# Weaving the P V of an older tile into the scores of a newer one, piece by piece, in a decode attention kernel

## The chip, the cores and the metric

The kernel runs on one core of a Trainium2 chip. The metric is the device time of one execution in microseconds (us), as the median of several executions. Engines carry the names of the profile: PE is TensorE (matmuls), PEld its weight loads, DVE VectorE, ACT ScalarE, SP SyncE, which here only issues transfers (DMAs).

## The reference, cut to what matters

One decode step: four sequences, 32 heads, 8192 cached keys and values of 128 numbers for each, in bf16. K and V together are 537 MB, and every byte is read once.

```python
B, Sq, D = 4, 1, 512
H, Sk, Dh = 32, 8192, 128
...
q = (x @ wq).reshape(B, Sq, H, Dh).transpose(0, 2, 1, 3)
scores = einsum("bhqd,bhkd->bhqk", q, k_cache) * (Dh ** -0.5)
p = softmax(scores)
o = einsum("bhqk,bhkd->bhqd", p, v_cache)
return x + o.transpose(0, 2, 1, 3).reshape(B, Sq, H * Dh) @ wo + FFN(layernorm(x))
```

## The kernel before

K and V come in 32 tiles each of 8.39 MB (four heads of one sequence). A tile fills one of three large slots. VectorE transposes a K tile in 32 pieces, TensorE multiplies each piece twice (64 matmuls of 512 columns a tile: the scores), and later multiplies P by V in 64 chunks of 512 columns (P V). The weights of a score matmul are 128 rows by 128 columns, those of a P V matmul 128 rows by 16 columns; every matmul loads its own.

```python
NSLOT = 3
slots   = ctx.enter_context(tc.tile_pool(name="slots", bufs=NSLOT))
kt_pool = ctx.enter_context(tc.tile_pool(name="ktp", bufs=3))
# ... (cut)
def t_piece(n, g, jb):                      # VectorE: one piece of K turned
    kt = kt_pool.tile([P, w // 2], dt.bfloat16, name="kt")
    nc.vector.transpose(out=kt[:]..., in_=src[:, :, jb, :])

def s_piece(n, g, jb):                      # TensorE: its scores, two matmuls
    for r in range(2):
        mm(s_ps[n][:], zq[:, 2 * jb + r, off:off + P], kt[:, :, r], ...)

def pv_chunk(n, k):                         # TensorE: one chunk of P V
    w = HT * NV                             # 16 columns of weights
    mm(o_acc[j % 2][b * QB:b * QB + w, :], pt[n][:, off:off + (w - 1) * QB + 1:QB],
       v_tiles[n][:, k * 512:(k + 1) * 512], start=(k == 0))
# ... (cut)
for i in range(NT):
    for g in range(NTG):
        for jb in range(2):
            t_piece(i, g, jb); s_piece(i, g, jb)      # all scores of tile i
        if g == 1 and i > 0:
            pt_turn(i - 1)                            # P of the tile before, transposed
    # ...
    load_v(i)                # into the slot that K(i) leaves
    max_1(i); build_q(i + 1)
    for k in range(NK):
        pv_chunk(i - 1, k)   # then all of P V of tile i - 1
        if k == 8:
            max_2(i)         # maximum, exp
    row_sums(i)
    load_k(i + 2)            # into the slot that V(i - 1) leaves
    if bv == B - 1:
        fin_1(jv); fin_q(jv) # every fourth tile: division by the row sums
```

## Time and profile before

| | before |
|---|---|
| median of the timed runs | 1304.13 us (1302.58 to 1304.63) |
| span in the profile | 1305.5 us |
| DMA share and rate, 2 to 1189 us | 1.00, 431 GB/s |
| PE busy | 87% of the span |
| mean spacing of K loads, tiles 4 to 31 | 39.3 us |
| two transfers of 8.39 MB at 431 GB/s | 38.9 us |

The two last rows are nearly equal: a stage (one tile's scores and one tile's P V) takes as long as its bytes. The prediction below shows the lines for that. One place in the same trace, which it does not show, became important afterwards. It is the change from scores to P V in the timeline of the kernel before (columns: start, duration, engine, line, operation, output and input, count, and in brackets the idle time before it and what ended it):

```profile
720.12 1.20 PE L75 MATMUL sps<-kt,zq 128*128 128x512 bf16 x4
...
720.71 0.10 PEld L75 LDWEIGHTS <-zq 128*128 128x128 bf16 x1 [0.27 <-issue]
721.25 1.64 PEld L75 LDWEIGHTS <-ptz 128*16 128x16 bf16 x9 [0.44 <-issue]
721.25 2.13 PE L75 MATMUL oacc<-slot,ptz 128*16 128x512 bf16 x9
```

Inside a run of one kind the matmuls start 0.216 us apart, and the next weights are loaded while a matmul runs. At the change the first weight load of P V starts at 721.25, together with its own matmul, 0.44 us after the load before it had ended. The records under these lines give starts of 720.934 for the last score matmul, 721.249 for the first P V matmul and 721.489 for the second: 0.315 and 0.240 us. So the change costs 0.315 + 0.240 - 2 x 0.216 = 0.12 us.

### The profile page before, as it was taken

The numbers are of one execution on the slowest core, as the hardware profiler recorded it, in microseconds if no ns is written. First come the engines' busy times: TensorE is split into PE (matmuls) and PEld (weight loads), VectorE is DVE, ScalarE is ACT, GpSimd is POOL, SyncE is SP. The second block draws the span as 40 slices with busy tenths as digits, with TensorE's granted clock in tenths as the row PEclk, the third lists the DMA queues.
The fourth block names the chain that finished last, engine by engine and source line by source line (L and its number), as shares of the span: only waits on it lengthen the run. The fifth ranks groups of instructions, "written<-read, shape, count | busy, mean of one in ns | idle before, by whom it ended". The sixth has DMA issues, their size and how long they took to land.

```text
span 1305.5 us, 12271 instructions
## 1 busy us (share of the span) xinstructions
PE 1136.1 (87%) x4725; PEld 463.8 (36%) x4788; DVE 807.9 (62%) x1509; ACT 35.0 (3%) x79; POOL 3.6 (0%) x11
## 2 busy tenths in 40 slices
PE   1898888988889988889988889988889988889889
PEld 0244333333333333333333333333333333333335
DVE  3956555676555676555676555686555776555771
ACT  1000000000000000000000000000000000000000
POOL 1000000000000000000000000000000000000000
PEclk9897999889989899899998899988999889989899
DMA  9999999999999999999999999999999999999985
GB/s 418 418 432 438 432 432 436 428 442 420 446 422 442 428 436 430 436 430 434 432 436 427 428 424 438 424 432 432 414 436 432 430 428 424 436 436 406 409 339 227
DMA packets 12466, 551.56 MB, mean 422 GB/s; under 512 B 1260, under 2 KB 1784, under 8 KB 3064
## 3 DMA queue, kind: packets, MB, share of 16 engines
q1 hardware_dynamic: 12392, 550.77, 98.1%
q8 instruction: 37, 0.61, 0.2%
q14 instruction: 21, 0.17, 0.0%
q10 hardware_dynamic: 16, 0.01, 0.0%
HBM read 550.77 MB, written 0.00 MB: 422 GB/s over the span
## 4 chain that ended last, share of the span: by engine, by line
PE 58%; DVE 20%; issue 18%; DMA 2%; ACT 0%; DVEq 0%; SPq 0%
PE oacc L75 34%; PE sps L75 21%; DVE kt L272 14%; DVE ptz L309 5%; DMA slot<-in_A_k_cache_dram 2%; PE mps L75 1%; PE yo_ps L75 1%; PE xps L75 1%; DVE o L346 1%; PE mps L291 1%; DVE kt L344 0%; ACT kt L343 0%; DVE rcp L319 0%; DVE otn L366 0%; ACT p__385 L300 0%
## 5 line engine op out<-in xcount | busy, mean ns | idle before, releaser
L75 PE MATMUL sps<-kt,zq 128*128 128x512 bf16 x1985 | 635.4, 430 | 133.3 <-DVE kt L272 133.0
L272 DVE STREAM_TRANSPOSE kt<-slot 128x512 uint32<-128x512 uint32 x1024 | 629.5, 678 | 32.8 <-DMA slot<-in_A_k_cache_dram 12.5
L75 PE MATMUL oacc<-slot,ptz 128*16 128x512 bf16 x2016 | 446.9, 380 | 0.0
L75 PEld LDWEIGHTS <-zq 128*128 128x128 bf16 x2048 | 215.7, 105 | 543.4 <-issue 419.6
L75 PEld LDWEIGHTS <-ptz 128*16 128x16 bf16 x2016 | 206.6, 105 | 226.9 <-issue 13.7
L319 DVE RECIPROCAL rcp<-mps 128x4 f32<-128x4 f32 x32 | 5.9, 185 | 363.9 <-PE mps L75 363.9
L285 DVE TENSOR_REDUCE mx<-sps 128x1 f32<-128x512 f32 x32 | 22.1, 692 | 22.4 <-PE sps L75 22.4
L294 DVE TENSOR_REDUCE nm<-mps 128x4 f32<-128x64 f32 x32 | 7.2, 225 | 31.8 <-PE mps L291 31.8
L75 PE MATMUL xps<-rowy,o 128*32 128x4 f32 (+1 forms) x226 | 10.5, 204 | 15.3 <-DVE o L346 15.3
L263 DVE COPY zq<-qt 32x4 bf16<-32x4 bf16 x128 | 21.1, 165 | 1.3
L75 PEld LDWEIGHTS xps<-rowy,o 128*32 128x32 f32 (+1 forms) x226 | 9.8, 154 | 16.0 <-DVE o L346 16.0
L75 PEld LDWEIGHTS mps<-rowb,rs 128*128 128x128 f32 x64 | 9.7, 190 | 14.9 <-issue 12.9
L75 PE MATMUL mps<-rowb,rs 128*128 128x4 f32 x64 | 12.5, 266 | 1.7 <-ACT p__385 L300 1.7
L75 PEld LDWEIGHTS <-slot 128*128 128x128 bf16 (+1 forms) x274 | 11.7, 123 | 6.3 <-DVE slot L191 2.6
L344 DVE TENSOR_TENSOR kt<-kt,rowu 128x512 f32<-128x512 f32 x8 | 5.5, 693 | 11.2 <-ACT kt L343 10.4
L291 PE MATMUL mps<-ident_f,mx 128*128 128x128 f32 x32 | 10.3, 323 | 0.8 <-DVE mx L285 0.8
L291 PEld LDWEIGHTS mps<-ident_f,mx 128*128 128x128 f32 x32 | 4.3, 133 | 14.2 <-issue 12.9
L366 DVE TENSOR_TENSOR otn<-xps,rcp 32x16 bf16<-32x16 f32 x28 | 4.8, 170 | 7.2 <-PE xps L75 5.1
L75 PE MATMUL yo_ps<-slot,otn 128*4 128x256 bf16 x64 | 8.1, 290 | 0.3 <-DVE otn L356 0.3
L346 DVE TENSOR_REDUCE o<-kt 128x128 f32<-128x512 f32 x8 | 8.2, 1022 | 0.3
L343 ACT COPY kt<-oacc 128x512 f32<-128x512 f32 x8 | 4.7, 586 | 96.8 <-PE oacc L75 96.8
L75 PE MATMUL yo_ps<-slot,kt 128*4 128x256 bf16 x28 | 5.8, 402 | 1.6 <-DVE kt L235 1.6
(148 smaller groups left out, 180.0 us busy)
## 6 DMA issues: line engine op xcount, KB each, us to landing
slot<-in_A_v_cache_dram SPq DMA_DIRECT2D x5, 2048.0 KB, 16.4
slot<-in_A_wq_dram SPq DMA_DIRECT2D x1, 4096.0 KB, 12.2
slot<-in_A_v_cache_dram SPq DMA_DIRECT2D x1, 4096.0 KB, 15.8
slot<-in_A_wo_dram SPq DMA_DIRECT2D x1, 3584.0 KB, 19.7
slot<-in_B_w_gate_dram SPq DMA_DIRECT2D x1, 1792.0 KB, 23.7
slot<-in_B_w_up_dram SPq DMA_DIRECT2D x1, 1792.0 KB, 27.5
slot<-in_B_w_down_dram SPq DMA_DIRECT2D x1, 1792.0 KB
slot<-in_A_v_cache_dram SPq DMA_DIRECT2D x1, 1024.0 KB, 19.7
```

The source lines that it names most:

```text
L75: nc.tensor.matmul(out_ap, lhsT=lhsT, rhs=rhs, start=start, stop=True, skip_group_check=True, **kw)
L263: nc.vector.tensor_copy(out=zq[a * QB:(a + 1) * QB, :, XO + a * QB].rearrange("p (j r) -> p r j", r=2), in_=qt[a * QB:(a + 1) * QB, half, ...
L272: nc.vector.transpose(out=kt[:].bitcast(dt.uint32).rearrange("p (t r) -> p t r", r=QB), in_=src[:, :, jb, :])
L285: nc.vector.reduce_max(out=mx[:], in_=s_ps[n][:], axis=AX.X)
L291: nc.tensor.matmul(mps[:, 0:P], lhsT=nmx.pop(n)[:, 0:1].to_broadcast([P, P]), rhs=ident_f[:, :], is_transpose=True, start=True, stop=True, ...
L294: nc.vector.tensor_reduce(out=nm[:], in_=by_row(mps[:, 0:P]), axis=AX.X, op=ALU.max, negate=True)
L309: nc.vector.transpose(out=t_[y * QB:(y + 1) * QB, :, y, :, :].rearrange("p s u x -> p s (u x)"), in_=p_[y * QB:(y + 1) * QB, :].rearrange( ...
L319: nc.vector.reciprocal(out=rcp[j][:, :, b], in_=mps[:, P:P + HT])
L343: nc.scalar.copy(out=o_sb[:].rearrange("p u d -> p (u d)"), in_=o_acc[j % 2][:])
L344: nc.vector.tensor_tensor(out=o_sb[:], in0=o_sb[:], in1=rowu[:].unsqueeze(2).to_broadcast([P, NV, Dh]), op=ALU.mult)
L346: nc.vector.reduce_sum(out=o1[:], in_=o_sb[:].rearrange("p u d -> p d u"), axis=AX.X)
L366: nc.vector.tensor_tensor(out=otn[q0:q1, j * 4:j * 4 + 4, :], in0=xps[q0:q1], in1=r_[q0:q1, y, :].unsqueeze(1).to_broadcast([QB, 4, B]), o ...
```

## The change

The intent: TensorE and VectorE should both work all the time, and less work should stand behind the last byte. Each half of a tile's scores now runs beside half of the P V of an older tile. The first half of K(i) runs beside the rest of V(i-2), the second beside the first part of V(i-1). K(i+1) is issued in the middle of stage i, when V(i-2) has been read. The last V tile lies in halves in two slots, the first one behind wo.

```diff
-    for i in range(NT):
-        for g in range(NTG):
-            for jb in range(2):
-                t_piece(i, g, jb)
-                s_piece(i, g, jb)
-            if g == 1 and i > 0:
+    for i in range(NT - 1):
+        for p in pieces(i, 0, HP):
+            if i >= 3:
+                pv_to(i - 2, NK // 2 + 2 * p)
+            if i != 2 and i > 0:
+                if p == 4:
+                    max_2(i - 1)
+                if p == HP - 2:
+                    row_sums(i - 1)
+        if i >= 3:
+            load_k(i + 1)
+        for p in pieces(i, HP, NP):
+            if p == 2 and i > 0:
                 pt_turn(i - 1)
+            if i >= 2 and p > 2:
+                pv_to(i - 1, (p - 2) * (NK // 2) // (HP - 2))
 ... (cut)
+            load_v(i)
         max_1(i)
+        build_q(i + 1)
+        if i >= 3:
+            fin(i - 2)
 ... (cut: the first three tiles)
     n = NT - 1
+    pv_to(n - 2, NK // 2 + 12)
+    max_2(n - 1)
+    pv_to(n - 2, NK)
+    row_sums(n - 1)
+    fin(n - 2)
+    t_ = slot()
+    load_wo(t_)
+    v_from(n, t_, H * D, 0, (T // 4, T // 4))          # first half of the last V
+    for p in pieces(n, 0, NP):
+        if p == 4:
+            pt_turn(n - 1)
+        if p > 8:
+            pv_to(n - 1, (p - 8) * NK // (NP - 8))
+    t_ = slot()
+    v_from(n, t_, 0, T // 2, (64, 32, 16, 8, 8))       # second half
 ... (cut: same work behind it, wo of the earlier heads sooner)
```

`pieces` transposes and multiplies one piece of K and then hands back control, and `pv_to(n, k)` does the P V chunks of tile n up to chunk k. So after each piece (two score matmuls) come two P V matmuls, in the second half two or three. The turn of P, in what follows, is its transpose on VectorE.

More of the change, by code (lines that the diff above doesn't have):

```diff
@@ L97, in load_v, with v_from, v_cols @@
     def load_v(n, parts=(T,)):
+        t_ = slot()
+        v_from(n, t_, 0, 0, parts)
+    def v_from(n, t_, base, t0, parts):
         j, b = divmod(n, B)
-        t_ = slot()
         src = A_v_cache[b, j * HT:(j + 1) * HT, :, :].rearrange("h (p t) d -> (h p) (t d)", t=T)
-        c0 = 0
+        v_tiles[n, t0 * Dh] = (t_, base)
         for w in parts:
-            c1 = c0 + w * Dh
-            nc.sync.dma_start(out=t_[:, c0:c1], in_=src[:, c0:c1])
-            c0 = c1
-        v_tiles[n] = t_
+            nc.sync.dma_start(out=t_[:, base:base + w * Dh], in_=src[:, t0 * Dh:(t0 + w) * Dh])
+            base, t0 = base + w * Dh, t0 + w
+    def v_cols(n, c0, c1):
+        h0 = max(c for m, c in v_tiles if m == n and c <= c0)
+        t_, base = v_tiles[n, h0]
+        return t_[:, base + c0 - h0:base + c1 - h0]
     load_k(0)
@@ L243, with load_wo @@
     wo_t = []
-    def load_wo():
-        t_ = slot()
+    def load_wo(t_):
         n = (NB4 - 1) * 4
@@ L329, in pv_chunk @@
         mm(o_acc[j % 2][b * QB:b * QB + w, :], pt[n][:, off:off + (w - 1) * QB + 1:QB],
-           v_tiles[n][:, k * 512:(k + 1) * 512], start=(k == 0))
+           v_cols(n, k * 512, (k + 1) * 512), start=(k == 0))
     def pv_last(xps, t0, t1, start=False):
@@ L337, in pv_last @@
             off = p_off(k) + u * QB
-            mm(xps[:, :, B - 1], v_tiles[n][:, t * Dh:(t + 1) * Dh],
+            mm(xps[:, :, B - 1], v_cols(n, t * Dh, (t + 1) * Dh),
                pt[n][:, off:off + (HT - 1) * NV * QB + 1:NV * QB], start=(start and t == t0))
@@ L373 @@
     NK = T // NV
+    NP = 2 * NTG
     JL = H // HT - 1
-    KM = NK // 2
+    KM = 24
+    TL = 48
     wo_next, wo_ready = 0, 0
+    pv_at = {n: 0 for n in range(NT)}
     def wo_some(n):
@@ L383, in wo_some, with pv_to, pieces, fin @@
             n -= 1
+    def pv_to(n, k):
+        while pv_at[n] < k:
+            pv_chunk(n, pv_at[n])
+            pv_at[n] += 1
+    def pieces(n, p0, p1):
+        for p in range(p0, p1):
+            t_piece(n, *divmod(p, 2))
+            s_piece(n, *divmod(p, 2))
+            yield p - p0 + 1
+    def fin(n):
+        nonlocal wo_ready
+        j, b = divmod(n, B)
+        if b == B - 1:
+            fin_1(j)
+            fin_q(j)
+            wo_ready = (j + 1) * HT
+    HP = NP // 2
     build_q(0)
     load_v(0)
-    for i in range(NT):
-        for g in range(NTG):
-            for jb in range(2):
-                t_piece(i, g, jb)
-                s_piece(i, g, jb)
-            if g == 1 and i > 0:
+    for i in range(NT - 1):
[11 more added lines that the diff above has]
+            if p == 2 and i > 0:
                 pt_turn(i - 1)
+            if i >= 2 and p > 2:
+                pv_to(i - 1, (p - 2) * (NK // 2) // (HP - 2))
         if i == 0:
@@ L400 @@
         elif i == NT - 2:
-            load_wo()
-        elif i == NT - 1:
-            load_v(i, (64, 64, 64, 32, 16, 8, 8))
+            load_v(i, (T // 4,) * 4)
         else:
@@ L406 @@
         max_1(i)
-        if i + 1 < NT:
-            build_q(i + 1)
-        if i == 0:
-            max_2(i)
-            row_sums(i)
-            continue
-        jv, bv = divmod(i - 1, B)
-        for k in range(NK):
-            pv_chunk(i - 1, k)
-            if k == 8:
-                max_2(i)
-        row_sums(i)
+        build_q(i + 1)
+        if i >= 3:
+            fin(i - 2)
         if i == 1:
+            pv_to(0, 8)
+            max_2(1)
+            pv_to(0, NK)
+            row_sums(1)
             load_v(1)
@@ L424 @@
             load_k(3)
-        elif i == NT - 1:
-            pass
-        elif i == NT - 2:
-            load_v(NT - 2, (128, 64, 64))
-        elif i + 2 < NT:
-            load_k(i + 2)
-        if bv == B - 1:
-            fin_1(jv)
-            fin_q(jv)
-            wo_ready = (jv + 1) * HT
-    n = NT - 1
+    n = NT - 1
+    pv_to(n - 2, NK // 2 + 12)
[11 more added lines that the diff above has]
+            pv_to(n - 1, (p - 8) * NK // (NP - 8))
+    t_ = slot()
+    v_from(n, t_, 0, T // 2, (64, 32, 16, 8, 8))
+    max_1(n)
+    wo_some(2)
+    max_2(n)
+    wo_some(H)
     pt_turn(n)
-    wo_some(H)
-    for k in range(KM):
-        pv_chunk(n, k)
+    row_sums(n)
+    pv_to(n, KM)
     fin_1(JL)
     xps = x_tile()
-    pv_last(xps, KM * NV, T - 48, start=True)
+    pv_last(xps, KM * NV, T - TL, start=True)
     fin_2(JL, xps)
-    pv_last(xps, T - 48, T)
+    pv_last(xps, T - TL, T)
     fin_3(JL, xps)
```

## The prediction

One clause on the Trainium skill is cut from it: the figure it gave is stated on its page for DMAs issued from GpSimd, and those here are issued from SP. "Its Specifications" are those of the page named before the cut.

> **What bounds the kernel now.** I read the page first, then the DMA queue's own waits, then one stage of the timeline, then windows for the rate and for the end. The page:
>
> ```profile
> PE 1136.1 (87%) x4725; PEld 463.8 (36%) x4788; DVE 807.9 (62%) x1509; ACT 35.0 (3%) x79; POOL 3.6 (0%) x11
> ...
> DMA  9999999999999999999999999999999999999985
> GB/s 418 418 432 438 432 432 436 428 442 420 446 422 442 428 436 430 436 430 434 432 436 427 428 424 438 424 432 432 414 436 432 430 428 424 436 436 406 409 339 227
> ...
> q1 hardware_dynamic: 12392, 550.77, 98.1%
> ```
>
> The DMA engines are full until the last two slices. Per tile 2 x 8.39 MB must come in, 19.45 us for each transfer at the rate below, 38.9 us a tile. Windows of the whole saturated part and of the end:
>
> ```profile
> 2.00:1189.00 1187.00, 1030.87 (x4163) 416.29 (x4222) 749.01 (x1399) 31.01 (x71) 2.26 (x3) 0.92 1.00 431
> ...
> 1231.00:1291.00 60.00, 55.85 (x260) 25.58 (x261) 28.29 (x54) 1.56 (x4) 0.00 (x0) 0.97 0.88 355
> ```
>
> The last two columns are DMA share and GB/s: 1.00 and 431, then 0.88 and 355. So transfers set the pace to about 1189 us, and 15 to 20 us are lost behind that. Who starts the transfers:
>
> ```profile
> SPq L104 <- DVE kt L272: 687.4, 29, 26.4
> SPq L94 <- PE mps L75: 416.5, 28, 14.9
> ```
>
> A V load starts when the last transpose has read the K slot, a K load when the last P V matmul has read the V slot. There are three slots. Now scores (23.2 us) and P V (15.0 us) alternate, and a K load for tile i+2 is queued while the V load issued 15 us before is still moving, so the queue is never empty. One stage, with the costs that I need:
>
> ```profile
> 1194.36 0.32 PE L291 MATMUL mps<-ident_f,mx 128*128 128x128 f32 x1
> ...
> 1194.62 12.06 PE L75 MATMUL oacc<-slot,ptz 128*16 128x512 bf16 x55
> 1194.72 0.23 DVE L294 TENSOR_REDUCE nm<-mps 128x4 f32<-128x64 f32 x1 [1.00 <-PE mps L291]
> ...
> 1195.18 0.16 DVE L297 TENSOR_REDUCE nb<-nm 128x1 f32<-128x4 f32 x1
> ...
> 1206.60 0.38 PE L75 MATMUL mps<-rowb,rs 128*128 128x4 f32 x2
> ...
> 1207.12 2.46 DVE L272 STREAM_TRANSPOSE kt<-slot 128x512 uint32<-128x512 uint32 x4
> 1207.86 0.39 PE L75 MATMUL sps<-kt,zq 128*128 128x512 bf16 x1 [0.87 <-DVE kt L272]
> ...
> 1213.11 0.10 PEld L75 LDWEIGHTS <-zq 128*128 128x128 bf16 x1 [3.15 <-issue]
> 1213.50 0.15 PEld L75 LDWEIGHTS <-zq 128*128 128x128 bf16 x1 [0.28 <-issue]
> 1213.92 0.15 PEld L75 LDWEIGHTS <-zq 128*128 128x128 bf16 x1 [0.28 <-issue]
> 1214.35 0.15 PEld L75 LDWEIGHTS <-zq 128*128 128x128 bf16 x1 [0.28 <-issue]
> ```
>
> To be seen: a full 512-column matmul costs 0.219 us (12.06/55) at full clock; after the 2.86 us in which PE waits for the turn of P, they start every 0.427 us, half clock. Such slow runs stand in every stage, 6 to 13 matmuls long.
>
> **What the Trainium skill says.** "TensorE: Matmul & The Clock Gate", Part 1, gives two clock states, half after an idle window of about 3.4 us and full after a busy one, 426.7 against 215.7 ns for 512 columns: the trace agrees (0.427, 0.219). "DMA: Bandwidth & Descriptors", Anatomy of one DMA, gives about 2 us fixed per DMA beside the bytes; here the 4096 KB of wq landed 12.2 us after issue, 9.7 us of it bytes at 431 GB/s, so 2.5 us at an empty queue. Its Specifications give a ceiling of 435 GB/s; 431 is measured, so the rate has no more to give. The first page's table calls VectorE's queue strict first in, first out; the trace agrees where a transpose starts only after the reciprocal ahead of it (1207.02, then 1207.12).
>
> **The change part by part.** No instruction is added or removed that matters: the same 4096 big matmuls, 1024 transposes and bytes. What moves:
>
> 1. Scores and P V share PE piece by piece. Compute alone gets shorter: 128 x 0.218 = 27.9 us of PE per tile, DVE 32 x 0.63 + 2.8 + 2.3 = 25 us beside it, in place of 38.2 us. But that is worth nothing in the middle, where 431 GB/s already binds.
>
> 2. The slots are held longer. V of tile i-2 is now read to the end of the first half of stage i, K of tile i to the end of the second. In the first half K(i) and V(i-2) hold two slots and V(i-1) is being filled; in the second K(i) and V(i-1) hold two, and K(i+1) is being filled. So no transfer waits behind the moving one until the half's compute is over. The first half starts when K(i) lands and must end, and the issue of K(i+1) reach the DMA engines, before V(i-1) is through: 19.45 us.
>
> 3. The first half, from K(i) landed to the last P V chunk: first transpose to first matmul 0.76; 64 matmuls x 0.218 = 13.95; the maximum after piece 4 sits in both orders, so PE waits from 1194.36 to the end of nb (0.98) plus one transpose of 0.67 and 0.09 of hand-over, 1.74; the row sums after piece 14 likewise, 1206.60 to 1207.86, 1.26. Before, the maximum cost PE nothing, being hidden amid P V. Sum 17.7 us. Then the clock: PE has waited 3 us or more for K(i), so it starts at half speed; about 10 matmuls x 0.21 = 2.1 to 2.3. Together 19.9 us, 19.2 at the least, 20.6 at the most.
>
> 4. To that come landing and restart of an empty queue, 1.4 to 2.5 us, I take 1.7. 19.9 + 1.7 - 19.45 = 2.15 us of empty DMA queue in each stage. K loads of this kind are K(4) to K(31), 28: 60 us lost.
>
> 5. The second half isn't critical: turn of P 2.9 us, then 60 matmuls, 13.1 us, and cold ones 2; its V load is freed by DVE, which runs up to three pieces ahead, some 16 us after V landed.
>
> 6. The end gets better. If DMA stayed full, 550.77 MB at 431 is 1278 us, plus 2 for the start and 2 for wo (4 MB in small rows, some 350 GB/s): 1282 us. wo and half of the last V go in at once, one slot earlier, and after the last 256 KB only a few small matmuls, the division, eight wo products, the casts and the store remain, 4.5 us by the trace (1300.97 to 1305.5) plus landing, 6.5. That would be 1288.5 in place of 1305.5: -17 us, of which 8 are dips between 1190 and 1271 and 9 the PE work behind the last byte.
>
> Sum: 1305.5 - 17 + 60 = 1348 in the profile, some 1.4 less timed, 1347. I shade it to 1344 for the rivals, most of which lie below.
>
> **Rivals.** (a) DMA stays full and only the end counts: 1287 us. It needs the first half under about 17.8 us. For it: without cold matmuls the first half is 17.7. Against it: a full DMA leaves PE some 4 us idle before every K, and 2.9 us sufficed to cool it. Middle cases give 1300 to 1330. (b) The restart costs the full 2.5 us: 1369. (c) PE stays at half clock for whole halves: 64 x 0.427 = 27.3 us, the half would last 31, 10 us lost a stage, some 1600 us. Against it: every slow run in the trace ends after at most two or three windows of dense work. (d) More than 2% faster needs under 1278 us, below the 1282 that the bytes take: practically closed.
>
> **Range and chances.** The loss per stage runs from 19.2 + 1.4 - 19.45 = 1.15 to 20.6 + 2.5 - 19.45 = 3.65, 32 to 102 us, but the extremes of both terms seldom meet, so 1320 to 1362 from this alone; I stretch the low end to 1290 because the whole loss is a small difference of two large numbers and (a) stands just below it. Over 2% slower is above 1330.2: 0.71. Within 2%: 0.26. Faster: 0.03.
>
> **What would show it.** DMA share about 0.95 and about 410 GB/s in the middle, dipping once a stage, just before a K load's issue; a K load issued some 41 us after the one before it, in place of 39.25; big waits of DVE's transposes on K's landing (now 12.5 us in all) of 2 to 5 us a stage; 0.43 us matmuls at the start of each first half; PE gaps of 1.3 us after the maximum and 0.9 after the row sums. The end: under 9 us from the last V byte to the last instruction, against 15. If DMA is 1.00 in the middle, step 4 is wrong and (a) holds; if the gap is there but first halves take under 19 us, the restart was dearer than I took; if PE never slows, step 3's clock term is wrong.

## The result, and the profile after

| | before | after |
|---|---|---|
| median of 4 runs each, same chip and rounds | 1304.38 us | 1497.72 us (1494.22 to 1507.21) |
| ratio | | 1.149, 95% interval 1.144 to 1.154 |
| span in the profile | 1305.5 us | 1505.4 us |
| mean spacing of K loads, tiles 4 to 31 | 39.3 us | 46.2 us |

A ratio is the mean time of one kernel's fast runs over that of the other's fast runs of the same rounds, so it is not quite the ratio of the medians quoted. The result is correct. The change made the kernel slower as predicted, but by 193 us, where 40 had been predicted, and the upper end of the range was 1362. The profile after is that of the slowest of the changed kernel's executions (1507.21 us; the others 1494 to 1498), so stage figures of single profiles are compared to some 0.3 us only.

These lines of the page of the changed kernel answer to those the prediction shows of the kernel before:

```profile
PE 1242.3 (83%) x4812; PEld 322.9 (21%) x4812; DVE 858.5 (57%) x1509; ACT 34.9 (2%) x79; POOL 3.6 (0%) x11
...
DMA  9999888988897988978988789887899778898794
GB/s 418 420 435 433 352 348 363 391 362 363 363 389 337 417 363 364 391 333 361 420 347 351 309 363 418 377 347 309 363 391 420 333 305 340 387 417 347 296 414 201
...
q1 hardware_dynamic: 12536, 550.77, 86.2%
...
PE 60%; DMA 28%; DVE 10%; issue 2%; DVEq 0%; ACT 0%; SPq 0%
...
slot<-in_A_k_cache_dram SPq DMA_DIRECT2D x32, 22.6
```

The same bytes keep the queue busy for 86.2% of the span instead of 98.1%. The line after that is the chain of work that ended last: transfers of K now make 28% of it, where they made 2% before. So the chain runs in turns through PE's work and through a K load, and the two no longer lie beside each other. The last line is the median time of a K load from issue to landing, 22.6 us. One stage by windows (columns: window, its length, busy time of PE, PEld, DVE, ACT and POOL, the granted clock, DMA share and GB/s), around a K load issued at 713.66 us:

```profile
710.00:714.60 4.60, 3.73 (x15) 1.19 (x15) 3.41 (x7) 0.00 (x0) 0.00 (x0) 1.00 0.00 0
714.60:736.50 21.90, 17.91 (x61) 3.99 (x60) 12.84 (x22) 0.00 (x0) 0.00 (x0) 0.92 1.03 432
736.70:759.50 22.80, 19.84 (x68) 4.49 (x68) 12.26 (x22) 0.78 (x2) 0.00 (x0) 0.93 0.75 322
```

In the first window nothing moves for 4.6 us: V has landed, and K waits for its slot. In the second, K moves at the full rate, and behind it the first of V, issued at 731.74 (21.9 us at 432 GB/s are 9.5 MB, K has 8.4). The third is the first half of the next stage. V fills only its first three quarters (0.75), and again the queue runs dry. The queue's waits say for what:

```profile
SPq L94 <- PE oacc L75: 793.6, 28, 31.3
SPq L107 <- DVE kt L278: 526.9, 30, 28.7
```

All 28 K loads of the loop (line 94) wait for a P V matmul, 793.6 us in all, where before it was 416.5. The middle of one stage of the timeline shows what PE does in that time:

```profile
704.59 0.11 PEld L75 LDWEIGHTS <-zq 128*128 128x128 bf16 x2 [0.41 <-issue]
704.60 0.62 PE L75 MATMUL sps<-kt,zq 128*128 128x512 bf16 x2
705.15 0.13 PEld L75 LDWEIGHTS <-ptz 128*16 128x16 bf16 x2 [0.44 <-issue]
705.15 0.62 PE L75 MATMUL oacc<-slot,ptz 128*16 128x512 bf16 x2
...
705.70 0.11 PEld L75 LDWEIGHTS <-zq 128*128 128x128 bf16 x2 [0.41 <-issue]
705.70 0.62 PE L75 MATMUL sps<-kt,zq 128*128 128x512 bf16 x2
...
710.11 0.39 PE L75 MATMUL mps<-rowb,rs 128*128 128x4 f32 x2
...
711.37 0.61 PE L75 MATMUL sps<-kt,zq 128*128 128x512 bf16 x2 [0.87 <-DVE kt L278]
...
713.66 0.33 SPq L94 DMA_DIRECT2D slot<-in_A_k_cache_dram  x1
...
736.70 2.49 DVE L278 STREAM_TRANSPOSE kt<-slot 128x512 uint32<-128x512 uint32 x4 [0.86 <-DMA slot<-in_A_k_cache_dram]
```

A pair of matmuls starts every 0.55 us, not every 0.43. Each pair's weight load starts with its own matmul, as at the change from scores to P V before the change. No engine is waited for here: the bracket on PE is empty, and PE counts as busy all the time. This profile shows the loss only in the spacing of the starts, not in a wait. PE's share of busy time even looks healthy.

Where the 200 us of the two profiles lie: up to the issue of K(4) 20.2 us (166.96 against 146.75), the 27 stages from K(4) to K(31) 188.0 us (7.0 each), and the end after K(31)'s issue -8.3 us (90.5 against 98.8).

### The profile page after: what moved, and what is told of

Its sections match the earlier page's. It is cut to its first block, busy times and chain, and to the rows that moved or that the text cites. A ratio compares the mean times of both kernels' runs of the same rounds, so it can differ in the third digit from the quotient of the medians.

```text
span 1505.4 us, 12238 instructions
## 1 busy us (share of the span) xinstructions
PE 1242.3 (83%) x4812; PEld 322.9 (21%) x4812; DVE 858.5 (57%) x1509; ACT 34.9 (2%) x79; POOL 3.6 (0%) x11
## 3 DMA queue, kind: packets, MB, share of 16 engines
q1 hardware_dynamic: 12536, 550.77, 86.2%
## 4 chain that ended last, share of the span: by engine, by line
PE 60%; DMA 28%; DVE 10%; issue 2%; DVEq 0%; ACT 0%; SPq 0%
PE sps L75 29%; DMA slot<-in_A_k_cache_dram 28%; PE oacc L75 27%; DVE kt L278 5%; DVE ptz L315 2%; PE mps L75 1%; PE xps L75 1%; PE yo_ps L75 1%; PE mps L297 1%; DVE mx L291 1%; DVE o L352 0%; DVE zq L269 0%; DVE nm L300 0%; DVE rcp L325 0%; DVE nm L301 0%
## 5 line engine op out<-in xcount | busy, mean ns | idle before, releaser
L75 PE MATMUL sps<-kt,zq 128*128 128x512 bf16 x2048 | 669.6, 414 | 226.0 <-DVE kt L278 226.0
L278 DVE STREAM_TRANSPOSE kt<-slot 128x512 uint32<-128x512 uint32 x1024 | 679.6, 694 | 253.2 <-PE sps L75 209.6
L75 PE MATMUL oacc<-slot,ptz 128*16 128x512 bf16 x2008 | 630.7, 407 | 1.5 <-DMA slot<-in_A_v_cache_dram 1.5
L75 PEld LDWEIGHTS <-zq 128*128 128x128 bf16 x2048 | 141.2, 100 | 658.1 <-issue 598.1
L75 PEld LDWEIGHTS <-ptz 128*16 128x16 bf16 x2008 | 144.7, 111 | 452.1 <-issue 425.4
L297 PEld LDWEIGHTS mps<-ident_f,mx 128*128 128x128 f32 x32 | 4.3, 136 | 13.2 <-issue 12.3
L75 PE MATMUL sps<-slot,xnt_w 128*32 128x512 bf16 x32 | 3.6, 630 | 4.3 <-DMA slot<-in_A_wq_dram 4.3
## 6 DMA issues: line engine op xcount, KB each, us to landing
slot<-in_B_w_gate_dram SPq DMA_DIRECT2D x1, 1792.0 KB, 24.2
slot<-in_A_k_cache_dram SPq DMA_DIRECT2D x32, 22.6
```

The source lines that it names most:

```text
L75: nc.tensor.matmul(out_ap, lhsT=lhsT, rhs=rhs, start=start, stop=True, skip_group_check=True, **kw)
L278: nc.vector.transpose(out=kt[:].bitcast(dt.uint32).rearrange("p (t r) -> p t r", r=QB), in_=src[:, :, jb, :])
L297: nc.tensor.matmul(mps[:, 0:P], lhsT=nmx.pop(n)[:, 0:1].to_broadcast([P, P]), rhs=ident_f[:, :], is_transpose=True, start=True, stop=True, ...
```

## The experiments

The first theory, A: a stage is its first half (from the first transpose of K to the last P V of the older tile) and then the longer of the lone landing of the next K and the second half. The halves do not lie beside the landing, since all three slots are held. What makes the first half long is mostly the change of weights' shape at each pair. The main rival, B: PE has too much work in all, and a saving anywhere on PE shortens the time. Other rivals, where a recorded expectation names them, concern the clock, the stalls and the transfer itself. Stage figures below are means over tiles 5 to 29 from the trace: "first half" from the first transpose of a K tile to the issue of the next K load, "second" from there to the next first transpose. For the changed kernel they are 22.8 and 23.2, together 46.0 us. The 23.2 hide two kinds of stage. In 18 of the 24 the next K lands 22.4 us after its issue (21.6 to 23.4) and the first transpose comes at 22.6. In every fourth, the one with the division, it comes only at 25.1, since VectorE is still at the division (here a K load issued at 805.70):

```profile
827.92 0.69 DVE L350 TENSOR_TENSOR kt<-kt,rowu 128x512 f32<-128x512 f32 x1
828.64 1.02 DVE L352 TENSOR_REDUCE o<-kt 128x128 f32<-128x512 f32 x1
...
831.41 2.53 DVE L278 STREAM_TRANSPOSE kt<-slot 128x512 uint32<-128x512 uint32 x4
```

### P V in groups, first half or second half only

`e1_group_h1` does the P V of the first half in groups of eight after every fourth piece, so it has 8 changes of shape instead of 32. `e2_group_h2` does that to the second half alone.

```diff
 # e1                                          # e2
-            if i >= 3:                        -            if i >= 2 and p > 2:
+            if i >= 3 and p % 4 == 0:         +            if i >= 2 and p % 4 == 0:
                 pv_to(i - 2, ...)                              pv_to(i - 1, ...)
```

> The changed kernel with P V in groups of eight chunks after every fourth piece, in the first half of a stage alone: 8 changes between score and P V matmuls in that half in place of 32. Theory A (slot lock: the next K load waits for the first half, and each change of matmul shape costs 0.12 us because the new weights are loaded in the open): 24 x 0.12 = 2.9 us less on the loop per stage, 28 stages, 81 us less, about 1415 us. Theory B (PE's total work bounds the stage, wherever it lies): the same gain here, about 1415, so this run counts only together with the next one. Theory C (the switch is not what costs; the clock or the waits do): about 1497.

> The same grouping in the second half of a stage alone. Theory A: PE has some 2 us of idle time there before K lands, the K load doesn't wait for this half, so no change, 1490 to 1500 us. Theory B (PE's total work bounds the stage): the same gain as the grouping of the first half, some 80 us, about 1415.

Measured: 1450.74 us (ratio 1.112, 1.108 to 1.116) and 1497.95 us (1.148). The second kernel saves about as many changes as the first and gains nothing: theory B falls. Its profile shows two small effects that cancel in this sum: in the stages with the division the second part falls from 25.1 to 23.1 us, while the first half grows from 22.8 to 23.3, with more slow starts (8.0 instead of 6.7) after a longer wait of PE for K. In the other stages the second part stays at 22.5, as the landing of K sets it. The first gains 47 us, about 60% of what was hoped, since its first half went only from 22.8 to 20.8. The timeline of its first half tells why. After a group VectorE has only three turned pieces ready, and PE then runs at VectorE's pace, as the short wait of 0.21 shows:

```profile
722.78 4.26 DVE L278 STREAM_TRANSPOSE kt<-slot 128x512 uint32<-128x512 uint32 x7
...
724.12 1.80 PE L75 MATMUL sps<-kt,zq 128*128 128x512 bf16 x6 [0.21 <-DVE kt L278]
725.85 1.91 PE L75 MATMUL oacc<-slot,ptz 128*16 128x512 bf16 x8
727.70 2.04 PE L75 MATMUL sps<-kt,zq 128*128 128x512 bf16 x8
```

### The same order, P V weights as wide as those of the scores

`e3_wide_pv` keeps the order of the changed kernel and gives P V weights of 128 columns. The numbers are wrong (the P V of one sequence overwrites rows of the others). The comparison with the reference nevertheless called it correct, so that word says little about the attention part of this run.

```diff
-        mm(o_acc[j % 2][b * QB:b * QB + w, :], pt[n][:, off:off + (w - 1) * QB + 1:QB],
+        mm(o_acc[j % 2][:, :], pt[n][:, off:off + P],
            v_cols(n, k * 512, (k + 1) * 512), start=(k == 0))
```

> The changed kernel with P V's weights widened from 16 to 128 columns, so that both kinds of matmul use the array in the same shape; the output is wrong on purpose, the order and number of instructions are the same. If the 0.12 us at each change is the price of changing the array's shape (the weights of a differently shaped tile cannot be loaded behind the running matmul): pairs fall from 1.10 to 0.87 us per piece, 3.7 us less in the first half, 28 stages, some 100 us less, about 1395. If it is the price of going to another accumulator or of the semaphore waits: no change, about 1497.

Measured: 1395.13 us (1.069, 1.066 to 1.072), 103 us less with as many matmuls and more weights to load. Its timeline:

```profile
706.69 0.61 PE L75 MATMUL sps<-kt,zq 128*128 128x512 bf16 x2
706.92 0.32 PEld L75 LDWEIGHTS <-ptz 128*128 128x128 bf16 x2
707.14 0.59 PE L75 MATMUL oacc<-slot,ptz 128*128 128x512 bf16 x2
707.36 0.31 PEld L75 LDWEIGHTS <-zq 128*128 128x128 bf16 x2
707.57 0.61 PE L75 MATMUL sps<-kt,zq 128*128 128x512 bf16 x2
```

The weight load now begins 0.22 us before its matmul, and a piece takes 0.88 us (706.69 to 707.57) instead of 1.10. So what costs is the change between the shapes 128x128 and 128x16, not the order as such. The first half fell to 19.7, by 3.1 us; 32 changes x 0.117 us are 3.7, and some two more matmuls at half clock (8.9 slow starts instead of 6.7, about 0.5 us) make most of the difference. Which property of the shape it is, the number of columns or the range of output rows, this run does not part, since it changes both.

### Maximum and row sums out of the first half

`e4_early_max` takes the other two stalls out of the first half: the maximum moves to the end of its own stage, the row sums to just ahead of the turn of P.

```diff
-            if i != 2 and i > 0:
+            if i == 1:
                 if p == 4:
                     max_2(i - 1)
 ...
             if p == 2 and i > 0:
+                if i > 2:
+                    row_sums(i - 1)
                 pt_turn(i - 1)
 ...
+        if i >= 2:
+            max_2(i)
```

> The changed kernel with the maximum and exponential of a tile moved to the end of its own stage, into the wait for K, and the row sums moved behind the middle of the next stage. Theory A: the two stalls of 1.74 and 1.26 us leave the first half, 3.0 us a stage, 84 us in all, about 1413 us; PE's gaps before the fifth and fifteenth piece are gone. If these stalls are hidden in another wait (the clock recovers during them or K comes no sooner): less than 20 us gained.

Measured: 1467.04 us (1.124). The first half shrank by 3.05 us to 19.8, which is what the two stalls had been sized at (1.74 + 1.26), but only 30 us of the total came back: the second part grew from 23.2 to 25.0 (22.6 to 23.8 in ordinary stages, 25.1 to 28.8 in those with the division). Its timeline names the growth, PE's wait for the row sums and the turn, 3.75 in place of 2.75, with PE at half speed behind it:

```profile
704.57 2.49 DVE L278 STREAM_TRANSPOSE kt<-slot 128x512 uint32<-128x512 uint32 x4
...
705.33 0.63 PE L75 MATMUL sps<-kt,zq 128*128 128x512 bf16 x2 [3.75 <-DVE kt L278]
...
706.86 1.03 PE L75 MATMUL sps<-kt,zq 128*128 128x512 bf16 x2
```

The gain was not lost: the second half, which had been hidden by the landing of K, had become the longer of the two. Theory A allows this, but I had expected the landing to stay the limit.

### Groups in both halves, with the early maximum

`e6_group4_early` puts the edits of `e1`, `e2` and `e4` together.

> The changed kernel with P V in groups after every fourth piece in both halves, and with the early maximum and late row sums of the run before. Alone, the first gave a first half of 20.8 us for 22.8, the second 19.8, where the second half (its end 25.0 us after the K issue, against 22.7 for the landing) took over as the limit. Theory A, made precise: a stage is the first half plus the longer of K's landing (22.7) and the second half. Together: first half 17.8, second half by grouping 3 us shorter, some 21.5, so stage 40.5 in place of 46.0 us, 28 stages, about 1344 us. If gains don't add up (other waits of the first half take over): about 1420.

Measured: 1373.88 us (1.053). First half 17.5, second part 24.2, DMA share 0.95. The expectation was missed by 30 us. In ordinary stages it came true: 17.5 + 23.1 = 40.6 us, where 40.5 was said, with K now issued 1.5 to 4.3 us before V has landed. In every fourth stage the division makes the second part 27.3, and there alone the queue still runs wholly empty (17.9 us over 24 stages in the DMA records, 118 for the changed kernel). Against the expected 22.7 that is 4.6 us in each of 7 stages, 32 us: the division, which the expectation left out, is about the whole miss.

### The clock

`e5_warm` puts 12 spare matmuls ahead of each first half, to have PE at full clock when K lands; `e9_warm2` puts 10 at the end of each stage that read only a tile which is ready.

```diff
+    def warm():
+        dps = psM.tile([P, 512], dt.float32, name="mps")
+        for _ in range(12):                       # e9: 10, weights from ptz
+            mm(dps[:], zq[:, 0, 0:P], ptz[:, 0].rearrange(...), start=True)
```

> The changed kernel with twelve spare 512-column matmuls (2.6 us, result unused) put into PE's wait for K at the start of each stage, so that the clock stays up. In the changed kernel some 6.7 matmuls of a first half run at half clock, 0.21 us each: 1.4 us. Theory A with the clock as one term of the first half: 1.4 us less on the loop per stage, 28 stages, about 1458 us, and no 0.43 us matmuls at the start of first halves. If the clock is hidden elsewhere, or the spare work delays the half as much as it warms: 1490 to 1505.

> The clock again: in the run with twelve spare matmuls these waited for a copy on VectorE and held the first half back by 1.4 us on the mean, as much as the clock gave. Here ten spare matmuls (2.2 us) read only data that is there, and run right at the stage's end, in PE's wait for K. If the half clock costs 1.4 us of a first half on the loop: about 1458 us. If not: 1490 to 1505.

Measured: 1505.11 us (1.154) and 1479.61 us (1.134). The first was flawed. The slow starts of the first half did fall from 6.7 to under 2, but the spare matmuls read the weights that VectorE writes just then, so they waited and delayed the real ones:

```profile
739.65 1.90 DVE L278 STREAM_TRANSPOSE kt<-slot 128x512 uint32<-128x512 uint32 x3
739.68 2.70 PEld L75 LDWEIGHTS <-zq 128*128 128x128 bf16 x14 [1.13 <-DVE zq L269]
739.68 2.76 PE L75 MATMUL mps<-ptz,zq 128*128 128x512 bf16 x12 [0.64 <-DVE zq L269]
742.28 0.61 PE L75 MATMUL sps<-kt,zq 128*128 128x512 bf16 x2
```

Without them the first score could have run about 0.76 us after 739.65; it ran at 742.28. The second form, free of that, takes 1.0 us from each first half (21.9) and 18 us from the total, half of what was expected; its first halves still have 1.6 slow starts. The clock is a real term, but of about 1 us a stage, and it is not the cause of the miss.

### The old P V first, then the K load

`e7_pv_first` does the rest of the older P V in one block ahead of the scores and issues K(i+1) right behind it. The changes of shape in the second half, all stalls and the clock stay. V(i-2) holds its slot for a short time only; the 32 changes of shape of the first half go as well.

```diff
+        if i >= 3:
+            pv_to(i - 2, NK)
+            load_k(i + 1)
         for p in pieces(i, 0, HP):
-            if i >= 3:
-                pv_to(i - 2, NK // 2 + 2 * p)
 ...
-        if i >= 3:
-            load_k(i + 1)
```

> The changed kernel with the rest of the older tile's P V done at the start of a stage, before any piece of K, and the next K load issued right behind it: the V slot is no longer held through the half. All other parts as in the changed kernel. Theory A: the DMA queue is never empty; what is left is the engines' own chain, 7.0 of P V, 0.8 plus 16 x 0.63 of scores paced by DVE, 3.0 of stalls, 2.9 for the turn of P, 14 x 1.1 + 1 in the second half, 2 of slow clock, some 42 us a stage: about 1386 us, DMA share over 0.90, K issued before the previous V has landed. Theory D (three slots are too few for halves, whatever the order within a stage): the queue still runs empty once a stage, about 1495.

Measured: 1372.95 us (1.052, 1.049 to 1.055), 125 us less than the changed kernel and a little better than expected. The K load is issued 6.7 us after the first transpose instead of 22.8, and the window of the middle shows the rate return:

```profile
200.00:1150.00 950.00, 815.08 (x3143) 263.44 (x3188) 589.97 (x1063) 21.43 (x52) 0.00 (x0) 0.95 0.95 405
```

For the changed kernel the same window has 0.86 and 366. So the slots decide whether the queue is filled, as theory A says. A rival in which the transfers had been slow for another reason would have left the rate where it was. How much of the 125 us is due to the slot and how much to the changes of shape that vanish with it, this run does not part.

### The new end on the old middle

`e8_tail_only` has the kernel before up to tile 30 and the end of the changed kernel (with P V in groups of four pieces), in three rounds.

> The kernel before, unchanged up to tile 30, with the new end alone: wo and half of the last V in one slot, the last tile's scores beside the P V of tile 30 (after every fourth piece). By the prediction's end term the dips in the DMA queue (8 us) and the PE work behind the last byte (9 us) shrink: 1288 to 1292 us if all of it comes, 1296 to 1300 if PE's work behind the last scores (PV, wo products, 64 of the last chunks) stays the limit. If the end of the change gains nothing without the halves in the middle: 1304.

Measured: 1302.26 us, ratio 0.9986 (0.996 to 1.001), the same. The 17 us that the prediction credits to the end are not there. The last bytes come only some 2 us sooner, and behind the last scores PE still has a chain of its own, as the timeline shows:

```profile
1279.77 5.84 PE L75 MATMUL yo_ps<-slot,otn 128*4 128x256 bf16 x52
1285.54 0.38 PE L75 MATMUL mps<-rowb,rs 128*128 128x4 f32 x2
1285.86 5.37 PE L75 MATMUL oacc<-slot,ptz 128*16 128x512 bf16 x24
1291.16 3.08 PE L75 MATMUL xps<-ptz,slot 128*128 128x4 bf16 x112
```

### Loads in halves, and the repaired change

`e10_kv_halves` cuts each K and V load into two DMAs of half a tile, so that the transposes can begin when half of K has landed. Nothing else is changed.

```diff
-        nc.sync.dma_start(out=t_[:], in_=A_k_cache[...])
+        src = A_k_cache[...]
+        for c in (0, SLOT // 2):
+            nc.sync.dma_start(out=t_[:, c:c + SLOT // 2], in_=src[:, c:c + SLOT // 2])
 ...
-    def load_v(n, parts=(T,)):
+    def load_v(n, parts=(T // 2, T // 2)):
```

> The changed kernel with each K and V load cut into two DMAs of half a tile, nothing else: the first half of a stage then waits only for the first half of K, the second only for the first half of V. Theory A (each half waits for the landing of a whole transfer that was itself issued behind the last half): the landing leaves the loop, PE's own chain stays, first half 21.4 without slow clock plus second half 20.7 plus 0.8, some 43 us a stage, about 1410 us, DMA share above 0.90. If the slots alone were the lock (three slots, one being filled), whatever the size of the transfers: about 1495.

Measured: 1450.24 us (1.112). That is 40 us above the expectation. K loads are 44.5 us apart, and the share of the DMA is 0.89. The landing of a whole K no longer stands between two stages, but now PE's own chain, with its changes of shape in both halves, does. `e11_kv_halves_g4e` therefore adds groups and early maximum to the halves, in three rounds.

> Halved loads together with P V in groups of four pieces and the early maximum: PE's chain is then 16 to 17.5 for the first half and 21.7 for the second, 38 to 39 us a stage, as much as the bytes take at 431 GB/s (38.9). Theory A: DMA share 0.98 or more from tile 5 on, 1290 to 1315 us, level with the kernel before or a little under it. If the switch and the stalls still bind: 1350 or more.

Measured: 1322.49 us (1.014, 1.012 to 1.017), just above the expected 1290 to 1315. Ordinary stages take 38 to 39 us, as long as their bytes. Every fourth stage takes 45, the one with the division, where PE waits at the end of the stage and the next scores wait with it:

```profile
732.34 1.02 DVE L354 TENSOR_REDUCE o<-kt 128x128 f32<-128x512 f32 x1
...
733.41 1.44 PE L75 MATMUL xps<-rowy,o 128*32 128x4 f32 x32 [4.16 <-DVE o L354]
```

`e12_best` moves the division into the second half, where scores lie around it, and does the old P V in larger groups early in the first half, in five rounds. Against `e11`:

```diff
             if i >= 3 and p % 4 == 0:
-                pv_to(i - 2, NK // 2 + 2 * p)
+                pv_to(i - 2, min(NK, NK // 2 + 11 * p // 4))
 ... (second half; its P V in groups of eight from the fourth piece on)
+            if i >= 3 and (i - 2) % B == B - 1:
+                if p == 6:
+                    fin_1((i - 2) // B)
+                if p == 12:
+                    fin_q((i - 2) // B)
 ...
-        if i >= 3:
-            fin(i - 2)
```

> The repaired form of the change: K and V loads in halves, early maximum, P V in groups (the rest of the older P V front-loaded, 11 chunks at each of pieces 4, 8 and 12), and the division of a finished group of four tiles moved from the end of a stage into its second half. Theory A (a stage is the first half plus the longer of second half and landing, and a queue that always has a transfer waiting hides the half): all stages take 39 us, DMA share 1.00 to the end, and the shorter end stays: 1288 to 1302. If the stages with the division still lack PE work (they took 45 us in the run before, waits of 4.2 us for the division and 3.8 us for the turn), 1305 to 1320. If the end gives nothing, as in the run with the new end alone, 1302 to 1306 even with a full DMA. More than 2% faster than before (under 1279) contradicts 431 GB/s and is expected by no theory.

Measured: 1300.96 us (1299.45 to 1301.80) against 1305.55 for the kernel before on the same chip, ratio 0.9964 (0.995 to 0.998). The window of the middle and the loads of one stage:

```profile
200.00:1150.00 950.00, 811.39 (x3318) 311.76 (x3379) 612.31 (x1126) 22.18 (x54) 0.00 (x0) 0.95 1.00 431
```

```profile
738.48 0.80 SPq L96 DMA_DIRECT2D slot<-in_A_k_cache_dram  x2
...
776.79 0.81 SPq L96 DMA_DIRECT2D slot<-in_A_k_cache_dram  x2
```

The queue is full again (1.00 and 431), and a K load follows the one before it after 38.3 us. Stages with the division take 41 to 43 us, as before the change. The loss of the change is gone entirely, with its idea kept. What is won over the kernel before is 0.4%: small, but the interval leaves 1 out. It lies at the end: 87.5 us from K(31)'s issue in the profile, against 98.8, less 3.3 us by which that issue comes later (1210.05 against 1206.70), most of it in the first tiles. From the landing of the last V to the end it is 5.7 us there, 13.2 before. The two profiles are 8.0 us apart, the medians 4.6.

## Why the prediction was right or wrong, by its own steps

1. That sharing PE is worth nothing in the middle was right: even the repaired kernel runs at 431 GB/s and no faster.

2. That slots are held longer, so that K(i+1) cannot be queued behind V(i-1), was right, and it is the mechanism of the loss in the middle. The windows show the empty queue, the queue's waits name the P V matmul, and `e7` takes away the lock, with the first half's changes of shape, and most of the loss.

3. The first half was to last 19.9 us and lasts 22.8. This is the step that failed, by one term of its sum: "64 matmuls x 0.218 = 13.95". Alternating in pairs, a piece takes 1.105 us, and 16 pieces take 17.7, 3.7 more. `e3` removes it with the order unchanged. The other terms hold or are smaller: 0.77 to the first matmul; 1.65 for the maximum (743.31 to 744.96 in the timeline) where 1.74 was said; 1.26 for the row sums (710.11 to 711.37), as said; for the clock 6.7 slow starts x 0.21 = 1.4 where 2.1 to 2.3 was said. Summed: 0.77 + 17.7 + 1.65 + 1.26 + 1.4 = 22.8.

4. "Landing and restart of an empty queue" was taken as 1.7 us. In stages without the division K lands 22.4 us after its issue, 3.0 over its 19.45 us of bytes, and the next first transpose comes after 22.6: 1.4 us more a stage than said. The division, which the sum left out, delays that transpose to 25.1 in every fourth stage, on the mean 0.6 us more. So the mean is 23.2, 2.1 above the sum. With step 3 a stage is 22.8 + 23.2 = 46.0 where 19.9 + 1.7 + 19.45 = 41.05 was said. Over 27 stages the miss is 134 us: 78 from the first half, 38 from the landing, 17 from the division. It is multiplied by the stages since the loss was a difference of two large, nearly equal numbers: 2.15 us were predicted, and any error in either goes into it whole.

5. That the second half is not critical was right for three of four stages, and only by a little; in the fourth the division made it the limit by 2.6 us (25.1 against 22.6). In `e4` and `e10` it became the limit in ordinary stages too, as soon as the first half or the landing got shorter.

6. The end was to give 17 us and gives 8.3. The transfers of the last V were to be queued at once. In the trace its second half is issued from 1480.8 us on, when the last transpose (start 1480.05) has left K(31)'s slot; the windows there show the queue nearly empty (0.10) just before, and the last V lands at 1494.1, 11.3 us before the end, where under 9 was predicted (13.2 before; `e12` with its 5.7 reaches it):

```profile
1475.00:1480.00 5.00, 5.00 (x20) 1.24 (x20) 2.84 (x4) 0.00 (x0) 0.00 (x0) 1.00 0.10 43
...
1490.00:1495.00 5.00, 5.00 (x27) 2.58 (x26) 0.18 (x1) 0.00 (x0) 0.00 (x0) 1.00 0.50 194
```

The sum also left out the first tiles, in which the new order starts up: K(4) is issued 20 us later than before. Together: predicted 0 + 60 - 17 = 43 in the profile, measured 20 + 188 - 8 = 200.

Of the rivals, (a), the full queue, is refuted by the DMA share of 0.86, (d), over 2% faster, by the time. (b), a dearer restart, is right in kind and dearer still than it took. (c), half clock for whole halves, is refuted: slow starts number 6.7 of 64, and warming PE gains 18 us. Of the signs it named, the dip once a stage, the 1.3 and 0.9 us gaps and the slow first matmuls are there. "Big waits of DVE's transposes on K's landing" of 2 to 5 us are not: where the first transpose waits for K at all it is 0.6 to 2.8 us, mostly near 1.2, because the second half ends just before K lands.

The missing number stood in the trace of the kernel before: 0.12 us at each change from scores to P V, in each of the 31 places where it can be read (0.315 to 0.317 between the two starts). The prediction took a matmul's price from a long run of one kind and applied it to an order made of changes.

What stays open is why a weight load of another shape is not pulled ahead, and which property of the shape decides it. How much of the 20 us of the first stages belongs to which cause was not tested either.

## What to carry to other kernels

When a change interleaves two kinds of matmul, price the seam and not only the run: find one place in the old trace where the kinds meet, take the spacing of the starts there, and multiply by the number of seams. PE shows such a loss as busy time. When buffers are few, ask which transfer can be in the queue at each moment; if the next one waits for a buffer that compute still reads, compute and transfer add up instead of overlapping, and then every tenth of a microsecond in that compute counts once a stage. Loads in halves and work in groups repair that, but a stage that already runs at the rate of the transfers has only its end left to win.

## What the Trainium skill lacked or had wrong

- "TensorE: Matmul & The Clock Gate", Part 2, step 1, says that PE pulls weight loads ahead of running matmuls when row groups do not conflict or the load goes to the background weights. The runs agree inside a run of one shape (0.216 us a matmul with fresh weights each). "TensorEngine Tiling (Array Packing)", Key Properties, says that a change of tiling mode drains TensorE, but not what that costs; whether weights of 128x128 and of 128x16 are two modes in its sense, no run here shows. Where the two alternate, the next weights were not loaded ahead, at 0.12 us per change (1.10 against 0.88 us for two pairs).
- "TensorE: Matmul & The Clock Gate", "Back-to-back issue gap", gives some 131 ns as the sustained spacing for 512 columns. No run here went under 0.214 us; its formula for the isolated gap, 216 ns, is what long runs show.
- "DMA: Bandwidth & Descriptors", Anatomy of one DMA, gives about 2 us of fixed cost for a DMA issued from GpSimd. The 8.39 MB loads here, issued from SP at an empty queue, took 3.0 us beside their bytes on the mean (22.4 less 19.45).
- "Perfetto Trace Analysis", DMA Optimizations, says that splitting DMAs may let some start sooner, with the DMA engines mostly idle in view, and gives no figure for a full queue. There halves cost no rate: 431 GB/s with halves (`e12_best`), 431 with whole tiles.
